# A new step order for a linear-attention and MLP kernel, from a plan in which engines take turns on a PSUM bank

## The chip, the core and the metric

The kernel runs on one core of a Trainium2 chip. The core has five engines that run their own instruction streams in order: TensorE (PE in the profile; its weight loads are shown as PEld), VectorE (DVE), ScalarE (ACT), GpSimd (POOL) and SyncE (SP, which here only issues DMAs). Matrix products land in PSUM, eight banks of 512 fp32 columns for each of 128 partitions; DVE and ACT carry results from there to SBUF. The metric is the device time of one execution in microseconds (us).

## The reference

A recurrent attention in the manner of RWKV-6 over 4 batches, 8 heads, 768 steps and heads of 48, followed by a token-mixing MLP:

```python
for t in range(S):                       # state: (B, H, 48, 48)
    cur = einsum('bhd,bhe->bhde', u[None] * kt, vt)
    y[:, :, t] = einsum('bhd,bhde->bhe', rt, state + cur)
    state = wt[:, :, :, None] * state + einsum('bhd,bhe->bhde', kt, vt)
x = y.transpose(0, 2, 1, 3).reshape(B, S, 384)
W_tok = 1/sqrt(64) * einsum('bsd,btd->bst', x @ w_q, x @ w_k)
out = relu(einsum('bst,btd->bsd', W_tok, x)) @ w_out
```

Inputs and output are fp32. All inputs together are 19.7 MB, and the output is 4.7 MB.

## The kernel before

The sequence is cut into units of 256 steps, three for each batch, so n runs from 0 to 11. A unit has two chunks of 128 steps. For each unit the function `unit` writes down some sixty steps. These are the ones that the rest speaks of, with their keys in the plan:

- **Loads** wg, kg, rg, vg (384 KB each, four buffers each, SP). For the last batch (units 9 to 11) v is loaded at once, as vw, in two steps of two DMAs.
- **ln** (ACT): log of the decay. **cw** (PE): running sums of it by a triangular matrix. **ep, en** (ACT): exp of plus and minus that sum, read from PSUM.
- **k16, r16, v16**: casts to bf16 (mostly POOL; k16 and r16 can also go to ACT).
- **kT, rT** (PE): transposes of k and r. Both land in one pair of PSUM banks, `kr`. For units 0 and 1 (`FULL`, line 245) k fills one bank and r the other; for all others each chunk has a bank that holds both.
- **ks** (ACT or DVE): copy of transposed k to SBUF. **qT** = r times ks, **RT** = r times ep (DVE, both read the `kr` banks), **KT** = ks times en (POOL or DVE; for units 0 and 11, `DIRECT`, DVE from the `kr` banks).
- **dps, dd, Vd**: the diagonal term, by PE, a copy of 16 columns, and a product on POOL. **vp, VB**: v in the order of steps, by PE and a copy; in the last batch VB is a POOL cast from vw.
- **A** (PE): scores of a chunk; **AM** (DVE): scores times the mask, 128x1024. **kb, kd**: KT turned back, by PE, and copied with a factor. **sn, SB**: the state, by PE and DVE. **yi, ya** (PE): output from the state and from the chunk. **X** (DVE): y scaled, plus Vd.
- **xt, XT**: X transposed and copied; **qk, QK**: the two projections and their copy.

At the end of a batch the MLP follows: **T** = k^T x by PE and **TS**, its copy; then for each unit **mx** (PE), **rl** (relu, to SBUF), **fp** (PE, with w_out), **os** (copy to SBUF) and **st** (store). In unit 11 (`end`) and the MLP of the last batch several steps are done in halves, one for each chunk.

The order is not that of the program text. `Plan` (lines 34 to 166) holds the steps with, for each engine that could do one, a time in ns. `order()` walks through the plan in planned time: each engine takes its steps by `RANK` (line 171, one number for each step); `ALT` (line 207) names, step by step, the engine for those that have a choice. A step may start when its engine is free, its inputs have ended, and a PSUM bank or ring buffer is free. `order()` also picks the banks (line 126). The steps are then issued in that sequence, so the plan fixes each engine's order and the banks; waits between engines come from the accesses. Thirty more steps, **z** (line 949), are fillers: a 128x512 product of zeros on PE, or nothing where `ALT` says `e`. Nine such products also stand in `setup`.

`begun` (line 415) gives the planned time at which each engine is through with the set-up. Clearing of buffers (`pads`, `kdz`) and `us`, `idu`, `gk` are DVE steps of the plan's start; `ub` copies the transposed u.

Of the kernel before, what the change touches and what calls it, by code (L numbers as in the profile page):

```python
# [33 lines left out]
class Plan:  # L34
# [4 lines left out]
    LAND = 1950  # L39

# [6 lines left out]
    def add(self, key, engs, fn, after=(), buf=None, reads=(), lag=None, mode=0, behind=None):  # L47
        opts = {}
        for e, x in engs.items():
            x = x if isinstance(x, tuple) else (x, mode, None)  # L50
            own = (260 if e in "Ee" else 80) if lag is None else lag
            opts[e] = (e.upper(), x[0], own, x[1], x[2])
        e = next(iter(opts)) if len(opts) == 1 else next(self.alt, "")
        e = e if e in opts else next(iter(opts))
        eng, dur, own, mode, kind = opts[e]
        if kind is not None:
            buf.kind = kind
        s = dict(key=key, opts=opts, way=e, eng=eng, dur=dur, fn=fn, lag=own, mode=mode, rank=0,
                 behind=behind, after=list(after), buf=buf, reads=list(reads), i=len(self.steps))
        if buf is not None:  # L60
            if buf.filler is None:
                buf.filler = s
                s["fill"] = buf.kind
                if behind is None:
                    s["behind"] = self.last.get(buf.kind)
                if buf.kind in self.rings:
                    self.last[buf.kind] = s
            else:
                s["fill"] = None
                if behind is None:  # L70
                    s["behind"] = buf.filler
        else:
            s["fill"] = None
        for b in reads:
            b.readers.append(s)
        self.steps.append(s)
        return s
# [8 lines left out]
    def order(self):  # L86
# [12 lines left out]
        owners, moved, done, mode = [None] * 8, [], [], 0  # L99

# [5 lines left out]
        def start(s):  # L106
# [9 lines left out]
            if s["fill"] in ("w", "s"):  # L116
                two = s["fill"] == "w"
                at = [clear(x) for x in owners]
                end = 7 if two else 8
                t = max(t, min(max(at[x:x + 1 + two]) for x in range(end)))  # L120
                if t >= never:
                    return never, None

                def beside(x):
                    return (x > 0 and at[x - 1] <= t) + (x < end - 1 and at[x + 1 + two] <= t)
                x = min((x for x in range(end) if max(at[x:x + 1 + two]) <= t),
                        key=lambda x: (beside(x), x if two else -x))
                return t, (x, 1 + two)
            if s["fill"] is not None:
                ring, size = rings[s["fill"]], self.rings[s["fill"]]  # L130
                if len(ring) >= size:
                    t = max(t, clear(ring[-size]))
            return t, None

        def run(s, t, took):
            s["start"], s["end"] = t, t + took + s["lag"]
            free[s["eng"]] = t + took
            done.append(s)

        while True:  # L140
# [16 lines left out]
            run(s, t, s["dur"] + self.SWITCH * change)  # L157
# [14 lines left out]
    0, 0, 0, 0, 2, 6, 4, 8, 5, 1, 17, 0, 0, 21, 2, 1, 5, 11, 0, 0, 0, 1, 0, 0, 2, 0, 0, 3, 0, 0,  # L172
    1, 3, 3, 4, 3, 4, 2, 5, 3, 4, 12, 6, 14, 10, 7, 12, 9, 5, 19, 9, 23, 12, 9, 10, 21, 16, 20,
    15, 13, 7, 15, 13, 27, 18, 37, 23, 29, 30, 31, 33, 22, 51, 22, 84, 35, 5, 0, 0, 4, 0, 0, 6,
    0, 0, 7, 0, 0, 8, 6, 7, 22, 10, 11, 24, 26, 17, 20, 21, 19, 8, 28, 14, 34, 16, 13, 38, 24,
    48, 28, 32, 15, 40, 26, 52, 29, 50, 53, 57, 61, 33, 76, 31, 92, 38, 8, 0, 0, 9, 0, 0, 10, 0,
    0, 11, 0, 0, 13, 11, 12, 35, 18, 17, 39, 42, 19, 27, 25, 15, 14, 49, 21, 58, 24, 18, 56, 31,
    63, 34, 55, 30, 60, 32, 67, 72, 68, 74, 37, 83, 42, 93, 39, 97, 41, 101, 44, 106, 47, 48, 0,
    0, 103, 45, 121, 54, 49, 0, 0, 126, 56, 138, 64, 52, 0, 0, 12, 0, 0, 13, 0, 0, 14, 0, 0, 15,
    0, 0, 20, 16, 17, 54, 23, 25, 64, 65, 26, 35, 36, 20, 19, 71, 28, 75, 32, 22, 78, 39, 82,  # L180
    41, 77, 38, 80, 40, 85, 43, 88, 90, 89, 91, 46, 105, 54, 111, 50, 16, 0, 0, 19, 0, 0, 20, 0,
    0, 21, 0, 0, 27, 34, 23, 73, 30, 29, 87, 94, 44, 48, 47, 45, 24, 95, 40, 100, 43, 29, 107,
    55, 99, 50, 96, 49, 104, 52, 110, 56, 115, 119, 117, 116, 60, 133, 59, 153, 69, 18, 0, 0,
    22, 0, 0, 23, 0, 0, 24, 0, 0, 33, 25, 26, 86, 37, 36, 98, 102, 42, 51, 53, 28, 27, 108, 49,
    109, 48, 30, 120, 61, 113, 58, 112, 57, 118, 59, 124, 129, 128, 127, 65, 134, 60, 155, 70,
    172, 77, 176, 79, 190, 86, 53, 0, 0, 178, 81, 205, 94, 51, 0, 0, 187, 84, 212, 97, 50, 0, 0,
    25, 0, 0, 28, 0, 0, 26, 0, 0, 29, 0, 0, 46, 31, 32, 114, 52, 53, 123, 125, 62, 64, 63, 36,
    33, 130, 58, 139, 63, 41, 141, 72, 136, 70, 135, 69, 140, 71, 143, 73, 147, 151, 152, 149,
    78, 163, 78, 177, 80, 27, 0, 0, 30, 0, 0, 31, 0, 0, 32, 0, 0, 51, 34, 35, 122, 55, 57, 131,
    132, 66, 68, 67, 39, 37, 137, 61, 148, 76, 45, 154, 80, 158, 82, 144, 74, 150, 77, 159, 81,  # L190
    169, 171, 173, 175, 91, 188, 85, 194, 88, 34, 0, 0, 33, 0, 0, 35, 0, 0, 36, 0, 0, 62, 38,
    40, 145, 67, 66, 142, 146, 65, 75, 79, 43, 42, 157, 72, 160, 83, 49, 174, 90, 165, 85, 164,
    84, 167, 86, 181, 184, 182, 183, 93, 189, 96, 206, 96, 215, 99, 229, 104, 238, 110, 54, 0,
    0, 234, 106, 246, 113, 55, 0, 0, 235, 120, 249, 115, 56, 0, 0, 37, 0, 0, 38, 0, 0, 40, 0, 0,
    42, 0, 0, 44, 0, 0, 68, 44, 46, 161, 74, 73, 168, 170, 87, 89, 88, 48, 51, 193, 99, 53, 192,
    98, 179, 92, 180, 82, 191, 97, 195, 101, 200, 203, 201, 202, 103, 213, 98, 222, 102, 39, 0,
    0, 41, 0, 0, 43, 0, 0, 71, 47, 50, 166, 76, 75, 185, 186, 83, 95, 94, 52, 54, 196, 100, 57,
    198, 102, 204, 104, 197, 89, 207, 105, 211, 108, 216, 218, 219, 220, 113, 226, 103, 232,
    105, 45, 0, 0, 47, 0, 0, 46, 0, 0, 87, 55, 56, 199, 92, 90, 93, 91, 208, 209, 95, 110, 107,
    106, 111, 109, 58, 221, 101, 59, 60, 214, 112, 225, 115, 217, 100, 223, 114, 224, 227, 228,  # L200
    230, 231, 233, 116, 236, 107, 239, 241, 108, 119, 117, 237, 118, 240, 245, 109, 111, 242,
    243, 244, 112, 121, 247, 122, 124, 250, 252, 125, 127, 57, 0, 0, 58, 0, 0, 248, 123, 114,
    253, 254, 128, 117, 59, 0, 0, 60, 0, 0, 251, 126, 116, 255, 256, 118, 129, 119, 130, 120,
    61, 0, 0, 43, 11, 44, 47, 6, 9, 45, 69, 62, 156, 25, 66, 18, 14, 10, 16, 59, 79, 36, 70, 41,
    2, 7, 210, 162, 81, 1, 8, 46, 17,
]
ALT = ("DPAEAAADEAAPPDDEAAEAEAAPPAPEAADEDAAAAAAAAPPAPEAAEDEDAAPDDeAAEDEAAPPAPEAADEAAAAAAAAAPPDPE"
       "AAEDEAAPPDPeADEDEAAPPAPEADDEDAAAAAADAPPDPDeAEAAPPAPDeAeAAPPAAAEAADEDAAADDDDDDADADAADADEE"
       "EEEEEEEEEEEEEEEEEEEEEeEEEEEE")
# [5 lines left out]
def kernel(  # L215
# [238 lines left out]
    def unit(n, batch):  # L454
# [71 lines left out]
        for cs in fine:  # L526
# [11 lines left out]
            x = add(("ep", n, cs[0]), {"A": 190 + int(w_ * 0.837)}, f_ep, [cws], ep, [cw])  # L538
            y = add(("en", n, cs[0]), {"A": 172 + int(w_ * 0.835)}, f_en, [cws], en, [cw])
# [8 lines left out]
        def transposed(name, src, step, place):  # L548
            def f(e):
                o = at(kr, BF16)  # L550
                for hp in range(NP):
                    for j in range(2):
# [10 lines left out]
                       mode=0 if full else 1)  # L563

        def turned(place, c0=0, nc_=2):
# [6 lines left out]
            e, view(ks.tile, 0, [[512, 2], [1, 512]]), turned(0)), [kTs], ks, [kr])  # L572
# [5 lines left out]
                  [rTs, kss], qT, [kr, ks])  # L578
# [3 lines left out]
        for cs in fine:  # L582
# [9 lines left out]
            def f_KT(e, cs=cs):  # L592
# [5 lines left out]
                else:  # L598
# [3 lines left out]
                    [rTs] + [eps[c] for c in cs], RT, [kr, ep])  # L602
            if n in DIRECT:
                y = add(("KT", n, cs[0]), {"D": 150 + int(n4 * C * 0.524)}, f_KT,
                        [kTs] + [ens[c] for c in cs], KT, [kr, en])
# [179 lines left out]
        for c in range(2):  # L785
# [6 lines left out]
            yas[c] = add(("ya", n, c), {"E": 205}, f_ya, [AMs[c], VBs], ys[c], [AM[c], VB])  # L792
# [96 lines left out]
        pieces = 2 if end else 1  # L889
# [4 lines left out]
        for ii in range(NU):  # L894
# [3 lines left out]
            def f_mx(e, ii=ii, mx=mx):  # L898
                for dt in range(NK):
                    mm(at(mx)[:, ds(dt * U, U)], TS.tile[:, ds(dt * 128, 128)],  # L900
                       view(QK.tile, ii * QS, [[64, 2], [C, 2], [1, 64]]),
                       start=(dt != 1))
# [5 lines left out]
            for cs in halves:  # L908
# [4 lines left out]
                    view(at(mx), cs[0] * C, [[U, NK], [1, w_]])), [mxs], MX, [mx])  # L913
            for cs in halves:
                def f_fp(e, cs=cs, fp=fp, MX=MX):
                    for c in cs:
                        for kt in range(NK):
# [4 lines left out]
                              fp, [MX])  # L922
            parts = 2 if end and ii == NU - 1 else 1
            for cs in halves:
# [5 lines left out]
                    [fps[cs]], o, [fp]) for x in range(parts)]  # L930
# [61 lines left out]
```

## Time and profile before

| | us |
|---|---|
| median of 3 runs | 106.54 (104.78 to 107.14) |
| profiled execution | 106.06 |
| its span, first to last instruction | 104.4 |

| group of the profile | count | busy us | mean ns |
|---|---|---|---|
| AM (DVE, 128x1024) | 24 | 29.1 | 1215 |
| KT (POOL, 128x1024) | 8 | 17.1 | 2132 |
| fillers Z (PE, 128x512) | 38 | 13.2 | 453 |
| fp (PE, 128x384) | 72 | 13.4 | 326 |
| ks on ACT / on DVE | 7 / 5 | 7.1 / 3.4 | 1018 / 686 |
| k casts on POOL / on ACT | 10 / 1 | 8.7 / 0.9 | 867 / 855 |
| os on ACT, 128x768 | 9 | 7.3 | 807 |

All DMA queues moved 24.66 MB; the queue of the loads and stores took 85.4% of the 16 DMA engines' time. The granted TensorE clock was 0.991 over the span.

How to read it: times are from one execution. A busy share says how much of a stretch an engine had an instruction running; a wait is idle time of an engine just before an instruction, put down to whatever ended last of the things it needed. A PE row ends when its pipeline has drained, so rows overlap, and the distance between starts is the better price of a step in a full stretch. On DVE and ACT too the next row starts up to about 0.1 us before the last one ends.

### The profile page before, as it was taken

How to read it: one execution, taken by the hardware profiler on the slowest of the kernel's cores; microseconds unless marked ns; L12 is line 12 of the kernel's file. 1: busy time of each engine (PE TensorE's matmuls, PEld its weight loads, DVE VectorE, ACT ScalarE, POOL GpSimd, SP SyncE). 2: the span in 40 equal slices, each digit the busy share in tenths (PEclk: the TensorE clock that was granted, in tenths of full speed). 3: DMA queues.
4: the chain of work that ended last, by engine and by line, in shares of the span. 5: the costliest groups of instructions: out<-in, count | busy, mean ns of one | idle time of the engine just before them, and what ended most of it. 6: DMA issues, size and time to landing. Idle time of an engine off the chain costs nothing.

```text
span 104.4 us, 4424 instructions
## 1 busy us (share of the span) xinstructions
PE 92.8 (89%) x1876; PEld 66.0 (63%) x1876; DVE 83.1 (80%) x145; ACT 80.4 (77%) x122; POOL 69.2 (66%) x80
## 2 busy tenths in 40 slices
PE   6999899979999998997998997999999879999920
PEld 2355568558577866675767865768686548766600
DVE  6256899598989999898998798899888497747820
ACT  6338896969799889996899759988989585765630
POOL 6486459896899859797979997396699705000000
PEclk9999999999999999999999999999999999999996
DMA  1999999999979999999979999999990039204693
GB/s 37 316 323 325 325 321 279 238 318 270 327 187 263 297 300 262 260 251 235 305 196 272 240 257 257 192 197 208 275 375 20 6 139 392 78 0 154 257 366 131
DMA packets 56403, 24.66 MB, mean 236 GB/s; under 512 B 54080, under 2 KB 55232, under 8 KB 56384
## 3 DMA queue, kind: packets, MB, share of 16 engines
q1 hardware_dynamic: 56224, 24.19, 85.4%
q8 instruction: 14, 0.23, 0.9%
q10 hardware_dynamic: 160, 0.20, 0.5%
q14 instruction: 5, 0.04, 0.1%
HBM read 19.66 MB, written 4.72 MB: 234 GB/s over the span
## 4 chain that ended last, share of the span: by engine, by line
PE 54%; POOL 11%; DVE 9%; ACT 8%; DMA 7%; issue 5%; SPq 2%; POOLq 0%; DVEq 0%; ACTq 0%
PE PS L254 54%; DMA vw<-in_v_dram 7%; POOL KT L600 5%; ACT ks L399 3%; DVE AM L687 2%; POOL Vd L667 2%; POOL r L490 2%; ACT kd L401 1%; DVE KT L600 1%; DVE ks L405 1%; SPq L307 1%; DVE X L804 1%; ACT en L535 1%; ACT ep L530 1%; SPq L314 1%
## 5 line engine op out<-in xcount | busy, mean ns | idle before, releaser
L687 DVE TENSOR_TENSOR AM<-PS,US 128x1024 bf16<-128x1024 f32 x24 | 29.1, 1215 | 0.8 <-PE PS L254 0.6
L667 POOL TENSOR_TENSOR Vd<-VB,dd 128x768 bf16<-128x768 bf16 (+1 forms) x14 | 18.5, 1325 | 7.0 <-issue 4.3
L600 POOL TENSOR_TENSOR KT<-ks,en 128x1024 bf16<-128x1024 bf16 x8 | 17.1, 2132 | 2.2 <-DVE ks L405 1.6
L535 ACT ACTIVATE en<-PS 128x1024 bf16<-128x1024 f32 (+1 forms) x14 | 12.4, 902 | 3.0 <-PE PS L254 2.6
L804 DVE SCALAR_TENSOR_TENSOR X<-PS,gx,Vd 128x768 bf16<-128x768 f32 (+1 forms) x13 | 12.4, 952 | 2.3 <-PE PS L254 2.1
L254 PE MATMUL PS<-Z 128*128 128x512 bf16 x38 | 13.2, 453 | 1.0 <-DVE Z L321 1.0
L254 PE MATMUL PS<-wo,MX 128*128 128x384 bf16 x72 | 13.4, 326 | 0.0
L530 ACT ACTIVATE ep<-PS 128x1024 bf16<-128x1024 f32 (+1 forms) x14 | 12.7, 924 | 0.5 <-PE PS L254 0.5
L254 PEld LDWEIGHTS <-KT 48*128 48x128 bf16 (+1 forms) x312 | 9.5, 94 | 4.8 <-issue 2.9
L479 ACT ACTIVATE lw<-wg 128x768 bf16<-128x768 f32 x12 | 10.2, 851 | 2.8 <-DMA wg<-in_w_dram 2.8
L590 DVE TENSOR_TENSOR RT<-PS,ep 128x1024 bf16<-128x1024 bf16 (+1 forms) x14 | 8.5, 606 | 4.0 <-ACT ks L399 2.6
L490 POOL CAST r<-rg 128x768 bf16<-128x768 f32 x12 | 9.9, 827 | 2.1 <-DMA rg<-in_r_dram 1.9
L490 POOL CAST k<-kg 128x768 bf16<-128x768 f32 x10 | 8.7, 867 | 1.9 <-DMA kg<-in_k_dram 1.0
L411 ACT ACTIVATE MX<-PS 128x768 bf16<-128x768 f32 (+1 forms) x10 | 7.5, 749 | 2.7 <-DVE MX L413 1.3
L399 ACT COPY os<-PS 128x768 f32<-128x768 f32 (+2 forms) x12 | 8.4, 698 | 1.5 <-PE PS L254 1.2
L254 PE MATMUL PS<-RT,KT 48*128 48x128 bf16 x192 | 9.4, 217 | 0.1
L254 PEld LDWEIGHTS <-MX 128*128 128x128 bf16 x72 | 6.5, 98 | 3.8 <-issue 0.2
L399 ACT COPY ks<-PS 128x1024 bf16<-128x1024 bf16 x7 | 7.1, 1018 | 2.4 <-DVE KT L597 1.2
L621 POOL CAST v<-vg 128x768 bf16<-128x768 f32 x9 | 7.5, 829 | 2.2 <-PE PS L254 1.1
L254 PE MATMUL PS<-CM,lw 64*128 64x128 bf16 x192 | 8.0, 224 | 0.4 <-DVE kd L407 0.4
L575 DVE TENSOR_TENSOR qT<-PS,ks 128x1024 bf16<-128x1024 bf16 x12 | 8.2, 681 | 0.3 <-PE PS L254 0.2
L254 PE MATMUL PS<-SB,RT 48*128 48x48 bf16 x160 | 7.0, 182 | 1.5
(89 smaller groups left out, 195.5 us busy)
## 6 DMA issues: line engine op xcount, KB each, us to landing
wg<-in_w_dram SPq DMA_DIRECT2D x12, 384.0 KB, 5.9
kg<-in_k_dram SPq DMA_DIRECT2D x12, 384.0 KB, 5.6
rg<-in_r_dram SPq DMA_DIRECT2D x12, 384.0 KB, 5.7
vg<-in_v_dram SPq DMA_DIRECT2D x9, 384.0 KB, 5.5
out_dram<-os SPq DMA_DIRECT2D x9, 384.0 KB, 3.2
vw<-in_v_dram SPq DMA_DIRECT2D x4, 288.0 KB, 6.0
out_dram<-os SPq DMA_DIRECT2D x5, 192.0 KB, 2.5
wof<-in_moe_w_out_dram SPq DMA_DIRECT2D x1, 576.0 KB, 6.2
```

Of the source, the lines that this page charges most:

```text
L254: return nc.tensor.matmul(o, l, rr, start=start, stop=stop, skip_group_check=True, is_transpose=trans)
L399: nc.scalar.copy(o, i)
L479: nc.scalar.activation(view(lw.tile, 0, [[64, H], [512, 2], [1, D]]), view(g["wg"].tile, 0, [[D2, H], [D, 2], [1, D]]), ACT.Ln, bias=0.0, ...
L490: op(view(o.tile, 0, [[64, H], [512, 2], [1, D]]), view(g[src].tile, 0, [[D2, H], [D, 2], [1, D]]))
L530: nc.scalar.activation(view(ep.tile, cs[0] * NP * EW + 66, [[EW, NP * len(cs)], [-65, 2], [1, 64]]), at(cw)[:, ds(cs[0] * 512, w_)], ACT.E ...
L535: nc.scalar.activation(en.tile[:, ds(cs[0] * 512, w_)], at(cw)[:, ds(cs[0] * 512, w_)], ACT.Exp, bias=0.0, scale=-1.0)
L575: lambda e: nc.vector.tensor_tensor(view(qT.tile, 0, [[512, 2], [1, 512]]), turned(second), view(ks.tile, 0, [[512, 2], [1, 512]]), ALU.mult),
L590: nc.vector.tensor_tensor(o, x, y, ALU.mult)
L600: x.tensor_tensor(o, view(ks.tile, cs[0] * 512, dims), y, ALU.mult)
L667: nc.gpsimd.tensor_tensor(Vd.tile[:, cols], VB.tile[:, cols], view(dd.tile, cs[0] * H, [[1, len(cs) * H], [0, D]]), ALU.mult)
L687: AMs[c] = add(("AM", n, c), {"D": 1221}, lambda e, c=c, A=A: nc.vector.tensor_tensor(view(AM[c].tile, 0, [[C, 8], [1, C]]), view(at(A), 0 ...
L804: nc.vector.scalar_tensor_tensor(view(X.tile, (2 * i + c0) * DM, [[DM, nc_], [1, DM]]), view(at(y), 0, [[512, nc_], [1, DM]]), gx, view(Vd ...
```

## The change

`Plan` is changed in five ways, and the step order and choice of engines were searched anew with it:

- A step that reads or writes a PSUM bank may, in the plan, only start when the other engines' last steps on that bank have ended (`used`, `banks`). `part` says which of a pair of banks a step touches, if only one.
- `OVER`: on ACT, DVE and POOL 100, 80 and 42 ns of a step's time are counted as overlapping the next step; its result comes as late as before, plus `AFTER`.
- `AFTER`: the time from a step's end to its users, by engine, in place of 260 for PE and 80 for all others.
- `COLD`: PE steps that start before 6,500 ns take twice as long in the plan.
- `RANK` and `ALT` have new values throughout.

Two edits change the instructions themselves. The copies that the last batch made in two pieces on two engines, TS and os of the last unit, are one piece again (os is still one for each chunk). And mx of the last batch writes its two chunks to two banks, as 18 matmuls of 128 columns in place of 9 of 256, where both chunks were spread over both banks before; relu reads accordingly.

```diff
+    COLD = 6500
+    OVER = dict(A=100, D=80, P=42)
+    AFTER = dict(E=200, A=80, D=62, P=65, S=80)
...
-            own = (260 if e in "Ee" else 80) if lag is None else lag
-            opts[e] = (e.upper(), x[0], own, x[1], x[2])
+            own = self.AFTER[e.upper()] if lag is None else lag
+            over = self.OVER.get(e, 0) if fn is not None else 0
+            opts[e] = (e.upper(), x[0] - over, own + over, x[1], x[2])
...
+        used = [{} for _ in range(8)]
+
+        def banks(s):
+            b = s["banked"]
+            if b is None or b.kind == "s" or s["part"] is None:
+                return [] if b is None else range(b.bank, b.bank + 1 + (b.kind == "w"))
+            return [b.bank + s["part"]]
...
+                t = max([t] + [y for x in banks(s) for e, y in used[x].items() if e != s["eng"]])
...
-            run(s, t, s["dur"] + self.SWITCH * change)
+            took = s["dur"] + self.SWITCH * change
+            run(s, t, took * (2 if e == "E" and s["fn"] and t < self.COLD else 1))
...
-        pieces = 2 if end else 1
+        pieces = 1
...
+                    x = TS.tile[:, ds(dt * 128, 128)]
+                    if end:
+                        for j in range(2):
+                            mm(at(mx)[:, ds(j * 512 + dt * C, C)], x,
+                               view(QK.tile, ii * QS + 64 * j, [[C, 2], [1, 64]]),
+                               start=(dt == 0))
+                        continue
...
-            parts = 2 if end and ii == NU - 1 else 1
+            parts = 1
```

What the new lists do, counted in the two built programs:

| step | before | after |
|---|---|---|
| ks on ACT / DVE | 7 / 5 | 2 / 10 |
| k16 on POOL (a half of unit 0 on DVE in both) / ACT | 11 / 1 | 7 / 5 |
| r16 on POOL / ACT | 12 / 0 | 11 / 1 |
| QK on ACT / DVE | 11 / 0 | 8 / 3 |
| XT on ACT / DVE | 9 / 4 | 11 / 2 |
| kd on ACT / DVE | 5 / 8 | 7 / 6 |
| rl on ACT / DVE | 10 / 5 | 8 / 7 |
| os on ACT / DVE | 12 / 5 | 14 / 1 |
| fillers z on PE / left out | 29 / 1 | 27 / 3 |

Among the orders that move: on DVE the k cast of unit 0 now stands ahead of `us`, `pads` and one `kdz`, and ks of unit 0 ahead of its KT. On PE one filler stands between kT and rT of unit 0, where six stood; the last filler is before rT of unit 3, where the last two stood among the steps of units 8 and 9. On POOL, KT of unit 10 comes before VB of unit 9, not after it. On SP, wg is loaded earlier against the other inputs, and the store of unit 3 comes before those of units 0 to 2.

## The prediction

> **What bounds the kernel now.** I read the busy shares first, then the stretches of the run, the waits of VectorE (DVE) between 7.5 and 75 us, the chain of waits, and the timeline of DVE at the start.
>
> The page's busy times (us, share of the span, instructions):
>
> ```profile
> PE 92.8 (89%) x1876; PEld 66.0 (63%) x1876; DVE 83.1 (80%) x145; ACT 80.4 (77%) x122; POOL 69.2 (66%) x80
> ```
>
> No engine is full over the span. By stretches (busy us of each engine, clock, DMA share, GB/s):
>
> ```profile
> 10.00:40.00 30.00, 28.27 (x641) 20.41 (x637) 27.39 (x40) 26.06 (x38) 24.08 (x24) 1.00 1.06 285
> 40.00:75.00 35.00, 32.29 (x775) 24.54 (x767) 31.55 (x47) 30.63 (x43) 28.99 (x25) 1.00 1.02 241
> 75.00:100.00 25.00, 23.27 (x416) 16.78 (x412) 18.57 (x34) 18.10 (x34) 9.44 (x9) 1.00 0.46 169
> 90.00:100.00 10.00, 9.88 (x87) 6.30 (x84) 6.67 (x14) 6.54 (x16) 0.00 (x0) 1.00 0.36 138
> ```
>
> Until 75 us TensorE (PE), DVE and ScalarE (ACT) are each some 90% busy: four in-order engines hand work to each other, and the stretch is as long as its fullest engine plus that engine's waits. PE's share there is flattered: 17 fillers (matmuls of zeros) stand after the first real A, about 0.22 us apart, and hide PE's waits. DVE, with no filler, has the least slack: 2.61 + 3.45 = 6.06 us. From 90 us on PE is full, and nothing but PE matters until its last matmul.
>
> What DVE waited for between 7.5 and 75 us (total us, times, longest):
>
> ```profile
> DVE RT L590 <- ACT ks L399: 1.5, 2, 1.1
> DVE RT L590 <- PE PS L254: 1.3, 2, 0.8
> DVE kd L407 <- PE PS L254: 0.9, 2, 0.5
> DVE X L804 <- PE PS L254: 0.8, 2, 0.4
> DVE kd L407 <- ACT kd L401: 0.5, 1, 0.5
> ```
>
> RT does not read ks. It reads the r half of the pair of banks whose k half ACT is copying into ks, so the first line is a wait for a turn on a bank. The end shows the same thing, beside the stretch that decides unit 9 (chain of waits; start us, us, what):
>
> ```profile
> 64.69 1.04 SPq L307
> ...
> 66.82 6.78 DMA vw<-in_v_dram
> ...
> 73.90 0.83 POOL VB L615
> 74.73 2.10 POOL KT L600
> ...
> 99.92 0.33 ACT os L399
> ...
> 100.27 0.36 DVE os L405
> ```
>
> The last two are the halves of one PSUM bank: DVE starts when ACT has ended. GpSimd (POOL) holds KT of unit 10 behind VB of unit 9, which waits for a load.
>
> The timeline of DVE at the start (start us, us; in brackets the idle time before it):
>
> ```profile
> 7.58 0.42 DVE L597 TENSOR_TENSOR KT<-PS,en 128x512 bf16<-128x512 bf16 x1 [0.95 <-ACT en L535]
> 9.53 0.42 DVE L590 TENSOR_TENSOR RT<-PS,ep 128x512 bf16<-128x512 bf16 x1 [0.83 <-PE PS L254]
> 10.81 0.42 DVE L407 TENSOR_SCALAR kd<-PS,gk 128x384 bf16<-128x384 bf16 x1 [0.45 <-ACT kd L401]
> 20.87 0.69 DVE L590 TENSOR_TENSOR RT<-PS,ep 128x1024 bf16<-128x1024 bf16 x1 [1.06 <-ACT ks L399]
> ```
>
> **The sum, on DVE.** The profiled execution took 106.06 us: a span of 104.4 and 1.66 around it, which I leave as it is. The median of the runs is 106.54, so the same change ends 0.5 us further from the median than from the profiled run. DVE's rows overlap, so I price a step by the distance of starts where DVE did not wait (AM 68.66 to 69.79: 1.13; ks 0.60; kd 0.54, its half 0.33; XT 0.47).
>
> *Waits that go.* (a) RT of unit 0 waited 0.83 for the r transposes, which stood behind six fillers (7.51 to 8.81 on PE); in the new order one filler stands between the k and the r transposes. (b) kd of unit 0: DVE takes the first half before ACT's, so the 0.45 falls on ACT. (c) ks of ten units is now on DVE, where it was on DVE in five; ACT keeps ks only for units 8 and 11. That removes RT's waits behind ks of unit 2 (1.06) and unit 10 (0.44). Together 2.78 us.
>
> *Waits that shrink.* The rest, 6.16 by the rows less 2.78, is 3.38 us, nearly all behind PE. PE in turn waited for DVE, ACT and POOL (SB 1.5, ks 0.5 and 0.3, kd 0.4, KT 0.3). POOL loses four k casts of 0.87 and one r cast of 0.83, 4.3 us of its 69.2, and does KT of unit 10 before VB of unit 9, so that the vw load no longer holds it. The bounds are 0 and 3.38; I take two thirds, 2.25, because POOL's lateness is what PE and the load slots hang on between 53 and 77 us.
>
> *Work that DVE gains*, units 0 to 10: four ks at 0.60 (2, 3, 5, 10; that of unit 0 is counted below); QK of unit 6, about 0.47 (an estimate by the XT copy of 0.47 and ACT's 0.48 for QK); relu of unit 2, 0.87 (row 0.95 less the overlap); two dd copies 0.16; kd of unit 9, 0.54. It loses three XT copies (1.41), three half kd (0.99), and pads and UB between KT and RT (0.46). Sum +1.58.
>
> *A wait that is added on DVE.* The k cast of unit 0 is now the first planned step and waits for its load (5.40 us as before). Behind it queue us, pads and one more clearing of kd, which lay in the idle time before 5.40. They are 0.25 + 0.42 + 0.68 = 1.35 us, so gk ends at 7.98 instead of 6.63; ks follows, and KT of unit 0 starts near 8.6 instead of 7.58: +1.0. A wait for ACT (0.95) gave most of the cover and is used up.
>
> *Casts on ACT.* ACT gains four k casts (0.86) and an r cast (0.84), two XT (0.80), two half kd, and loses five ks (1.02) and three QK (0.48): with os and relu about +0.1 of 80.4. Its sum costs nothing; the places might (second rival).
>
> *PE.* Two fillers fewer, 0.4 us, in idle time: nothing. The 256-wide matmuls of the last mx become 18 of 128 columns; equal columns, starts about 0.06 us apart as in the X transposes (six in 0.50) against 0.11: nothing. The ways of kb, vp and xt shift by a few matmuls: nothing.
>
> *The end.* os of the last chunk was 0.33, then 0.36, with a store behind both: 100.63 less 99.92 is 0.71. One ACT copy of 384 columns is 0.48: −0.22. ACT does all six last half copies; each PE group ahead takes 0.49, so it keeps up. TS in one piece instead of two turns saves as much, but lies behind fp of unit 7 (PE is full there): nothing. The stores' order changes, after all loads in both: nothing.
>
> Sum: −2.78 − 2.25 + 1.58 + 1.0 − 0.22 = −2.67, so 103.4 us.
>
> Which measure of PE is right bears on this. By the rows PE idles 11.6 us of the span and is full at the end. The Trainium skill (Perfetto Trace Analysis, "Identifying the Most-Contended Engine") calls matmul busy time a poor measure and takes that of weight loads: 63%, which would leave 38 us of slack and make a much larger gain possible. Between 90 and 100 us the trace disagrees: weight loads fill 6.30 us of 10, yet the matmuls stand back to back and carry the chain. I keep the rows.
>
> **Rivals.**
>
> *DVE becomes the bound (no change).* If PE-released waits merely return as other waits, only the named ones go: −2.78 + 1.58 + 1.0 − 0.22 = −0.4, 105.6. For it: DVE's 83.1 grows, and 40 to 75 us has only 3.45 idle. Against it: DVE is the chain for 9% only. It includes that the change does not do what it says: the build made the engines take turns already, and a re-ranked list that replaces each wait by an equal one gives 106.06.
>
> *Casts hold ACT (slower).* ACT is in order, and k of unit 2 now waits there for its load, with VB, ln, kd and en behind it, and through en and kd the whole unit. POOL's casts waited for loads up to 1.55 us (r), ACT's ln up to 1.8. At 1.1 us for each of five casts it is +5.5; against −2.67 that is +2.8: 108.9. It ends slower than before from 0.53 us a cast. Against it: from unit 3 on loads landed well before use, and wg now comes earlier in the queue.
>
> *All waits go.* Every DVE wait (−6.16), +2.58, −0.22, and PE's wait of 1.04 at 83 us behind SB: −4.8, 101.2.
>
> *The clock falls.* The last filler now stands before r of unit 3; before, two stood at 61 and 63 us. At the start eleven fillers take 4.87 us, 0.44 apart, twice the 0.22 of later ones: a PE that has not run is half as fast. If a wait sent it back for as long, 4.9 us would do the work of 2.4: +2.4, 105.8. From 35 to 100 us the longest wait of PE was 1.04 us and no row shows that pace again, with two fillers, so it hardly decides. The Trainium skill (TensorE: Matmul & The Clock Gate, "What's actually happening") names about 3.4 us of idleness for the fall; no run here shows one.
>
> **Chances.** Forecast 0.52, centre 103.4; DVE bound or nothing done 0.25; ACT held 0.10; all waits go 0.10; clock 0.03. About 2% (2.1 us; 104.4 and 108.7) is what can be told from no change here. The forecast's own range is 102.3 (all 3.38 go) to 104.9 (a quarter goes); about a sixth of its chance lies above 104.4. Faster: 0.43 + 0.10 = 0.53. Same: 0.09 + 0.25 + 0.03 (clock) = 0.37. Slower: 0.10. The range is 101.2 (all waits go) to 107.0 (the casts hold ACT by 0.72 us each, +3.6 − 2.67); it leaves out the held ACT at its full price and what lies below 101.2.
>
> **What would show it.** Right: no RT behind ks before unit 8; AM of unit 0 near 11.0 instead of 11.74 although KT starts later; DVE idle under 3 us between 10 and 75; KT of unit 10 well before 74.7; one os copy at the end. Wrong: DVE idle unchanged with other names, or ACT idle before k casts, released by DMA. What would overturn it: PE less busy than 9.5 of 10 us in the last stretch.

## The result and the profile after

| | before | after |
|---|---|---|
| median of 20 runs each, us | 105.34 (104.41 to 107.14) | 104.03 (103.26 to 105.5) |
| ratio after to before | | 0.9887, 95% interval 0.9851 to 0.9922 |
| profiled execution, us | 106.06 | 103.3 |
| its span, us | 104.4 | 101.6 |

The change makes the kernel 1.1% faster, within the 2% that count as no change. Ratios here and below leave out executions more than 1.5% above the fastest of the same kernel, the profiled one of before among them, while medians and ranges hold all. The two profiled executions are 2.76 us apart because that of before lies above its median and that of after below; typical executions are 1.2 to 1.3 us apart. A difference read between the two profiles must therefore be checked against other executions of the same order.

The page's busy times after (us, share of the span, instructions):

```profile
PE 90.9 (90%) x1881; PEld 65.5 (64%) x1881; DVE 84.2 (83%) x146; ACT 80.6 (79%) x123; POOL 64.9 (64%) x75
```

POOL has lost 4.3 us and five instructions, DVE has gained 1.1. By stretches of after (busy us of PE, weight loads, DVE, ACT, POOL; then clock, DMA share, GB/s):

```profile
10.00:40.00 30.00, 27.79 (x615) 19.71 (x614) 27.37 (x41) 24.78 (x35) 21.70 (x21) 1.00 1.07 290
40.00:75.00 35.00, 33.57 (x837) 26.05 (x830) 33.42 (x51) 33.64 (x48) 31.07 (x26) 1.00 1.05 252
75.00:100.00 25.00, 21.84 (x381) 16.25 (x379) 17.62 (x30) 16.94 (x33) 6.23 (x7) 1.00 0.49 186
```

From 10 to 40 us DVE is idle for 2.63 us, as before (2.61). From 40 to 75 us it is idle for 1.58 instead of 3.45. What DVE waited for between 7.5 and 75 us in after (total us, times, longest):

```profile
DVE ks L426 <- PE PS L275: 1.1, 3, 0.6
DVE SB L772 <- PE PS L275: 0.9, 2, 0.5
DVE AM L713 <- PE PS L275: 0.8, 2, 0.5
DVE qT L599 <- PE PS L275: 0.4, 2, 0.2
DVE RT L614 <- PE PS L275: 0.3, 1, 0.3
```

No line names ACT any more; all waits are now for PE. The start of the run in after, by the timeline of DVE:

```profile
8.04 0.68 DVE L426 COPY ks<-PS 128x1024 bf16<-128x1024 bf16 x1
8.64 0.41 DVE L621 TENSOR_TENSOR KT<-PS,en 128x512 bf16<-128x512 bf16 x1
8.97 0.41 DVE L614 TENSOR_TENSOR RT<-PS,ep 128x512 bf16<-128x512 bf16 x1
10.56 0.40 DVE L428 TENSOR_SCALAR kd<-PS,gk 128x384 bf16<-128x384 bf16 x1
10.95 1.22 DVE L713 TENSOR_TENSOR AM<-PS,US 128x1024 bf16<-128x1024 f32 x1
```

KT starts 1.06 later than before, and AM 0.79 earlier, with nothing idle between. And the chain of waits of after (start us, us, what):

```profile
10.15 6.02 DMA wg<-in_w_dram
...
16.25 0.85 ACT lw L500
...
25.61 0.09 DVE dd L426
...
25.84 1.47 POOL Vd L693
27.31 0.77 POOL v L647
28.08 1.26 POOL r L511
...
29.38 4.58 PE PS L275 x98
...
85.73 11.53 PE PS L275 x131
...
97.28 0.48 ACT os L420
```

The chain now runs from a load of unit 2 over POOL's Vd of unit 2, which waits for dd, to the cast of r of unit 3 queued behind it. The load vw and POOL's VB, on the chain of before from 65.7 to 74.7 us, are off it.

**Where the time went.** I cut the traces at three products AM, which every kernel has: the first in time of unit 5, the first of unit 10 and the last of unit 11. The table also holds the traces of the experiments below; "old" and "new" is the order of the steps, and in the last two rows steps of the new order are put back.

| trace | order | start to unit 5 | unit 5 to 10 | unit 10 to 11 | rest of span |
|---|---|---|---|---|---|
| before | old | 44.56 | 32.96 | 10.67 | 16.2 |
| b_again | old | 44.44 | 31.63 | 10.68 | 16.2 |
| b_half_v | old | 44.53 | 31.65 | 10.67 | 16.2 |
| b_pieces | old | 44.43 | 32.41 | 10.68 | 16.2 |
| b_ks_dve | old, ks moved | 44.26 | 32.22 | 10.17 | 16.2 |
| b_ks_dve_2 | old, ks moved | 44.22 | 33.10 | 10.18 | 16.2 |
| b_ks_pieces | old, ks moved | 44.87 | 32.13 | 10.17 | 16.0 |
| after | new | 44.77 | 31.12 | 9.63 | 16.1 |
| a_half_v | new | 44.96 | 31.67 | 9.63 | 16.1 |
| a_start | new | 44.94 | 31.91 | 9.63 | 16.1 |
| a_wg2 | new | 44.65 | 31.53 | 9.63 | 16.1 |
| a_wg2_r3 | new | 44.36 | 32.55 | 9.64 | 16.7 |
| a_ks_act | new, ks back | 49.75 | 31.52 | 9.66 | 16.6 |
| a_pool_casts | new, casts back | 51.15 | 32.12 | 10.82 | 15.9 |

Three things stand in it. Up to unit 5 the change gains nothing. From unit 5 to 10 the time varies by 1.4 to 1.5 us in either order, so the 1.84 us between the two profiles there cannot be told from two different executions. From unit 10 to 11 each order repeats to 0.01 us, and the new one is 1.04 shorter; of the last two rows one repeats the new order to 0.03, and the other, a_pool_casts, has lost the gain (see there). PE has about as much to do there: the profiles have 229 matmul records in that stretch in both, though not all of the same steps (before still holds the transposes of unit 11's k, after the sums cw of unit 11), and PE is busy for 9.41 us before and 9.31 after, so its idle time fell from 1.26 to 0.32. (Less fillers, the first stretch has some 19 records fewer in the new order and the second 11 more, so these two are compared to within a us.) With the last stretch (16.2 to 16.1) that makes 1.1 to 1.2 us, the difference of typical executions.

What happens between unit 10 and unit 11 is seen on DVE. Before (timeline of DVE; in brackets the idle time ahead and what ended it):

```profile
81.73 0.42 DVE L597 TENSOR_TENSOR KT<-PS,en 128x512 bf16<-128x512 bf16 x1 [0.28 <-PE PS L254]
83.29 0.42 DVE L590 TENSOR_TENSOR RT<-PS,ep 128x512 bf16<-128x512 bf16 x1 [1.14 <-ACT ks L399]
83.63 0.35 DVE L746 TENSOR_TENSOR SB<-PS,ep 128x192 bf16<-128x192 f32 x1
```

and of ACT and PE in the same execution:

```profile
82.25 1.01 ACT L399 COPY ks<-PS 128x1024 bf16<-128x1024 bf16 x1 [1.20 <-DVE KT L597]
...
84.03 0.49 PE L254 MATMUL PS<-ID,X 128*128 128x128 bf16 x6 [1.04 <-DVE SB L746]
```

DVE, ACT and DVE take turns on the banks of unit 11's k and r: ks waits for KT, RT waits for ks, SB stands behind RT, and PE has nothing to do for 1.04 us. After, ACT's copy, still on ACT, is ahead of en and long done (ACT, then DVE):

```profile
76.83 1.02 ACT L420 COPY ks<-PS 128x1024 bf16<-128x1024 bf16 x1
```

```profile
79.25 0.68 DVE L599 TENSOR_TENSOR qT<-PS,ks 128x1024 bf16<-128x1024 bf16 x1
79.85 0.42 DVE L621 TENSOR_TENSOR KT<-PS,en 128x512 bf16<-128x512 bf16 x1
80.18 0.79 DVE L614 TENSOR_TENSOR RT<-PS,ep 128x512 bf16<-128x512 bf16 x2
```

Nothing waits, and PE is busy for 11.71 of the 12 us from 78 to 90, where it was 10.52. Before first, then after:

```profile
78.00:90.00 12.00, 10.52 (x241) 7.91 (x241) 9.21 (x15) 9.06 (x16) 6.58 (x8) 1.00 0.38 145
```

```profile
78.00:90.00 12.00, 11.71 (x238) 9.10 (x231) 11.23 (x19) 7.93 (x14) 3.23 (x4) 1.00 0.24 90
```

### The profile page after: what moved, and what is told of

Same layout as the page of the kernel before. It is cut to its first block, busy times and chain, and to the rows that moved or that the text cites. A ratio compares the mean times of both kernels' runs of the same rounds, so it can differ in the third digit from the quotient of the medians.

```text
span 101.6 us, 4422 instructions
## 1 busy us (share of the span) xinstructions
PE 90.9 (90%) x1881; PEld 65.5 (64%) x1881; DVE 84.2 (83%) x146; ACT 80.6 (79%) x123; POOL 64.9 (64%) x75
## 4 chain that ended last, share of the span: by engine, by line
PE 57%; DVE 10%; SPq 9%; ACT 7%; DMA 6%; POOL 3%; issue 3%; DVEq 0%; ACTq 0%; POOLq 0%
PE PS L275 57%; SPq L328 9%; DMA wg<-in_w_dram 6%; DVE AM L713 5%; ACT lw L500 2%; POOL Vd L693 1%; DVE ks L426 1%; DVE qT L599 1%; ACT os L420 1%; POOL r L511 1%; ACT QK L420 1%; ACT ep L551 1%; DVE X L831 1%; DVE SB L772 1%; ACT XT L420 1%
## 5 line engine op out<-in xcount | busy, mean ns | idle before, releaser
L275 PEld LDWEIGHTS <-KT 48*128 48x128 bf16 (+1 forms) x304 | 10.0, 94 | 4.7 <-issue 2.7
L275 PE MATMUL PS<-Z 128*128 128x512 bf16 x36 | 11.9, 435 | 1.0 <-DVE Z L342 1.0
L420 ACT COPY os<-PS 128x768 f32<-128x768 f32 (+1 forms) x14 | 9.3, 663 | 2.7 <-PE PS L275 2.6
L420 ACT COPY XT<-PS 128x768 bf16<-128x768 bf16 (+1 forms) x11 | 8.5, 771 | 0.5 <-ACT en L556 0.2
L772 DVE TENSOR_TENSOR SB<-PS,ep 128x192 bf16<-128x192 f32 x20 | 7.0, 351 | 1.4 <-PE PS L275 1.4
L275 PE MATMUL PS<-CM,lw 64*128 64x128 bf16 x192 | 7.5, 217 | 0.8 <-ACT lw L500 0.8
L275 PE MATMUL PS<-VB,AM 128*128 128x48 bf16 x192 | 8.2, 184 | 0.0
```

The costliest lines, as they stand in the source:

```text
L275: return nc.tensor.matmul(o, l, rr, start=start, stop=stop, skip_group_check=True, is_transpose=trans)
L420: nc.scalar.copy(o, i)
```

## The experiments

Three theories stood against each other in turn. "Turns": the gain is that four copies ks, and with them DVE's turns behind ACT, leave ACT. "POOL relief" or "loads": it is that POOL's casts and the loads behind them leave the chain. "Search": it is the new order as a whole, and no part of it alone. All runs below are compared with the kernel before on the same chip.

Steps were moved by two lines in the plan, with a table of engines and ranks for the steps named:

```diff
-        e = e if e in opts else next(iter(opts))
+        e = WAY.get(key, e) if e in opts else next(iter(opts))
...
-            s_["rank"] = x
+            s_["rank"] = AT.get(s_["key"], x)
```

**b_again**, the kernel before unchanged, for a second trace.

> The kernel before, unchanged, profiled a second time. The first profile had a span of 104.4 us in a run of 106.06, while the median is now 105.34; there the eleven fillers at the start took 4.87 us and the first cw began at 5.84, in the profile of the changed kernel they took 4.18 and cw began at 5.14, though neither order nor number of these matmuls changed. Theory 'phase': the start differs from run to run; a second profile can show cw at 5.1 to 5.9 and the span follows by less than that, 103 to 104.5. Rival 'order': cw of unit 0 is late in the kernel before for a reason of its order, and starts at 5.84 again.

It took 104.78 us. At the start the same eleven fillers and the sums cw behind them ran faster (cw at 5.29 instead of 5.84 us), and AM of unit 0 came only 0.11 earlier for it: of the faster start little is left there. What differs most is POOL from 47 to 56 us. Before (POOL's timeline):

```profile
49.34 0.83 POOL L490 CAST r<-rg 128x768 bf16<-128x768 f32 x1 [0.36 <-DMA rg<-in_r_dram]
...
53.73 0.83 POOL L490 CAST k<-kg 128x768 bf16<-128x768 f32 x1 [0.70 <-PE PS L254]
54.52 2.14 POOL L600 TENSOR_TENSOR KT<-ks,en 128x1024 bf16<-128x1024 bf16 x1
```

and b_again, the same casts:

```profile
48.59 0.83 POOL L490 CAST r<-rg 128x768 bf16<-128x768 f32 x1
...
52.23 0.83 POOL L490 CAST k<-kg 128x768 bf16<-128x768 f32 x1
53.02 2.13 POOL L600 TENSOR_TENSOR KT<-ks,en 128x1024 bf16<-128x1024 bf16 x1
```

A load of r came late in one execution and not in the other, a cast behind it then waited for PE too, and KT is 1.50 us apart. (In that line the wait is put down to what came last.)

**b_pieces**: the kernel before in its old order, but TS and os copied whole, and the last mx in two banks.

```diff
-        Ts = [add(("TS", n, x), ..., lambda e, x=ds(x * w_, w_): copy(e, TS.tile[:, x], at(T)[:, x]), ...)
+        Ts = [add(("TS", n, x), ..., lambda e, x=x: x == 0 and copy(e, TS.tile[:, ds(0, DM)], ...), ...)
```

> The kernel before with the edits of instructions alone: TS and os of the last unit in one piece, mx of the last batch with a bank for each chunk, the old order. Theory (forecast): only the end of the last os matters, 0.71 us becomes 0.48, so -0.2 us of 105.3: ratio 0.998, and PE as full as before from 90 us on. Rival: the pieces and the mixed banks held PE up in the tail, and a good part of the 1.1% is here: ratio 0.992 or less.

0.9934 (0.9885 to 0.9982), between the two expectations. Its trace has the old 10.68 us from unit 10 to 11. From the last AM to the end of the last copy it has 12.10 us, where before has 12.44 and after 12.24, so the pieces are worth 0.2 to 0.3 us up to there. Little of this reaches the end: the rest of the span is 16.2 us as before. And the medians, 106.0 and 106.06, show no gain, so the 0.7% is not shown to be one.

**b_ks_dve** and its repetition **b_ks_dve_2**: the kernel before, old order, with four ks on DVE.

```diff
+WAY = {('ks', 2): 'D', ('ks', 3): 'D', ('ks', 5): 'D', ('ks', 10): 'D'}
+AT = {('ks', 2): 24.5, ('ks', 3): 33.5, ('ks', 5): 50.5, ('ks', 10): 93.5}
```

> The kernel before with ks of units 2, 3, 5 and 10 moved from ACT to DVE and nothing else. Theory 'turns': RT's waits for ACT's ks of units 2 and 10 (1.06 and 0.44 us) go, ACT loses 4 x 0.93 us, DVE gains 4 x 0.60; DVE loses 1.5 us of waits and gains 2.4 of work, ACT gets room: between -1.0 and +0.9 us, 0.3 faster if I must say one: ratio 0.997. Rival 'search': moving single steps without re-ranking the rest only shifts waits; DVE is the fullest engine, so +1 to +2.4 us: ratio 1.01 to 1.02.

> b_ks_dve once more (the kernel before with ks of units 2, 3, 5 and 10 on DVE, old order), since b_ks_pieces, which has it and more, measured 0.999 on another chip. If four ks on DVE are worth 1.1% by themselves: 0.985 to 0.993 again. If the 0.9893 was owed to a chip on which the kernel before is slow (its median there was 106.06, in the other comparisons 105.3 and 105.7), and the gain of the kernel after needs the new order: 0.995 to 1.002, about 105.0 us on any chip.

0.9893 (0.9838 to 0.9947) on one chip and 0.9991 (0.9916 to 1.0066) on another. The wait of RT behind ks of unit 2 is gone in both, and the first AM of unit 2 comes 0.67 and 0.70 us earlier than before; by unit 5, 0.30 and 0.34 are left, and by unit 10 the two are 1.04 and 0.20 ahead of the profile of before and both behind b_again. Why the first ratio is the lower one is not shown. Of the 17 executions of the kernel before that it is taken against none was under 105.43 us, though b_again took 104.78 on the same chip; on the other chip the fastest was 104.61. In unit 11, not edited, the turn fell otherwise: ACT copied ks ahead of KT. DVE's timeline of b_ks_dve_2:

```profile
82.49 0.42 DVE L601 TENSOR_TENSOR KT<-PS,en 128x512 bf16<-128x512 bf16 x1 [1.26 <-ACT ks L403]
82.84 0.41 DVE L594 TENSOR_TENSOR RT<-PS,ep 128x512 bf16<-128x512 bf16 x1
```

One wait in place of two, and the stretch from unit 10 to 11 is 10.18: half of the gain there without any new order. From the last AM to the end of the last copy both then take 12.68 us for the 12.44 of before, so half of that half is lost again. Alone, the four ks are worth little that can be told.

**b_ks_pieces**: both of these edits together.

> The kernel before in its old order and with its old engines, but for the two parts that measured best alone: ks of units 2, 3, 5 and 10 on DVE, and TS and os copied whole with two banks for the last unit's mx. If the two gains are separate, 0.9893 x 0.9934 = 0.983, below the kernel after (0.9887), and nothing of the gain is owed to the new order. If they are the same slack counted twice, 0.989. Rival 'search' (part of the gain is owed to the new order): 0.990 or more. The last copy out should take 0.48 us as in the kernel after, not 0.71.

0.999 (0.9912 to 1.0069). Not the sum of the two gains and not the gain of one; it goes with the second run of b_ks_dve. "Search" was nearest. The last copies out are as expected: three of them stand back to back in 1.41 us.

**a_ks_act**: the kernel after with the same four ks back on ACT.

```diff
+WAY = {('ks', 2): 'A', ('ks', 3): 'A', ('ks', 5): 'A', ('ks', 10): 'A'}
+AT = {('ks', 2): 18.5, ('ks', 3): 24.5, ('ks', 5): 40.5, ('ks', 10): 81.5}
```

> The changed kernel with ks of units 2, 3, 5 and 10 put back on ACT, nothing else moved. Theory 'turns': RT and qT wait again for a turn on the bank pair behind ACT's 0.9 to 1.0 us, and ACT, 33.64 us busy of 35 between 40 and 75 us, has no room: +1.0 to +2.5 us, ratio to before 0.998 to 1.01 (the changed kernel: 0.989). Rival 'ks is indifferent': DVE is relieved by 2.4 us and that pays for the turns: 0.985 to 0.993.

1.026 (1.0181 to 1.0339), slower than any theory had it. ACT is in order, and here ks of unit 5 (42.27 us, 1.01) went ahead of TS, for which PE waited. PE's timeline of a_ks_act:

```profile
43.72 0.50 PE L279 MATMUL PS<-QK,TS 128*128 128x256 bf16 x3 [1.49 <-ACT TS L424]
```

Then the clock fell (see the end). What an undone part costs is thus the price of a step out of place in an order made without it, not the worth of the part.

**a_pool_casts**: the kernel after with five casts back on POOL.

```diff
+WAY = {('k16', 2): 'P', ('k16', 3): 'P', ('k16', 7): 'P', ('k16', 11): 'P', ('r16', 4): 'P'}
+AT = {('k16', 2): 11.5, ('k16', 3): 13.5, ('r16', 4): 19.5, ('k16', 7): 29.5, ('k16', 11): 50.5}
```

> The kernel after, with five casts given back to POOL: k16 of units 2, 3, 7 and 11 (ACT and DVE have them in the kernel after) and r16 of unit 4, at the places of the old order. All else stays. POOL gets 5 x 0.83 = 4.15 us back, 64.9 to about 69 us. Theory 'turns' (the gain is that four ks left ACT's queue; b_ks_dve, which does that alone in the old order, measured 0.9893): POOL has slack, the ratio to the kernel before stays at 0.985 to 0.992, the place of the kernel after. Rival 'POOL relief' (the gain of the kernel after is that POOL is no longer on the chain with its casts, loads and KT from 53 to 77 us): back to 0.996 to 1.004. Rival 'fit' (a searched order and its engines belong together, so that one part undone costs whatever it is, as in a_ks_act with 1.026): over 1.005, with a wait in front of PE that neither kernel has.

1.0664 (1.0575 to 1.0753), with two new waits in front of PE ("fit"). Waits of PE in a_pool_casts:

```profile
PE PS L279 <- POOL r L515: 3.7, 2, 2.8
PE PS L279 <- POOL k L515: 2.1, 1, 2.1
```

On POOL the cast of k of unit 2 stands behind a cast of v that waited 1.68 us for its load, and that of r of unit 4 behind KT, which waited 2.32 us for DVE. The run says that the new order needs these casts off POOL, and nothing on whether the old one did.

The stretch from unit 10 to 11 is 10.82 us here, and its reason is a third wait. ACT still copies ks of unit 11 ahead of en, and DVE waits for no turn, but the cast of its k is late (POOL, then PE's weight loads):

```profile
83.46 0.83 POOL L515 CAST k<-kg 128x768 bf16<-128x768 f32 x1
```

```profile
84.34 0.29 PEld L279 LDWEIGHTS <-k 64*128 64x128 bf16 x16 [1.29 <-POOL k L515]
```

PE transposes k as soon as POOL has cast it, and had been idle for 1.12 us. In after ACT casts this k at 70.59. So in the new order the gain there also needs this cast early; b_ks_dve, with the cast on POOL, has half of it.

**a_start**: us, kdz and pads of DVE's start put back ahead of the first k cast.

```diff
+AT = {('us',): 0.4, ('kdz', 1): 0.5, ('pads',): 0.6}
```

> The kernel after, with us, kdz and pads of the start put ahead of DVE's k cast of unit 0, where the kernel before has them. My forecast charged their new place with 1.0 us. By it KT of unit 0 comes from 8.64 us to about 7.9, the first AM from 10.95 to about 10.3, and if that carries to the end the ratio is 0.981 to 0.984. Rival 'the start is bound by loads' (the chain of the kernel after runs from the tenth load, wg of unit 2, landed at 16.25 us): AM moves, the end doesn't, 0.985 to 0.992.

0.9891 (0.9823 to 0.9958), the place of the kernel after. KT came to 8.10, but RT then waited for en, and AM started where it had. In this execution PE's sums cw and with them the first en came 1.03 us later than in the profile of after (7.00 for 5.97), so the rows do not price the move; that nothing is gained at the end rests on the ratio. The timeline of DVE in a_start:

```profile
8.69 0.42 DVE L616 TENSOR_TENSOR RT<-PS,ep 128x512 bf16<-128x512 bf16 x1 [0.18 <-ACT en L558]
...
10.99 1.23 DVE L715 TENSOR_TENSOR AM<-PS,US 128x1024 bf16<-128x1024 f32 x1
```

**a_wg2** and **a_wg2_r3**: the kernel after with the load of wg of unit 2 one place earlier (and the k cast of unit 2 later on ACT), and the same with POOL's r cast of unit 3 ahead of Vd of unit 2.

```diff
+AT = {('wg', 2): 7.5, ('k16', 2): 14.5}                      # a_wg2
+AT = {('wg', 2): 7.5, ('k16', 2): 14.5, ('r16', 3): 14.5}    # a_wg2_r3
```

> The kernel after, with the load of wg of unit 2 issued one place earlier on SP, ahead of kg of unit 2, and that unit's k cast after its ln on ACT. If the load of wg sets the chain at the start, ln of unit 2 begins some 1.1 us before 16.25 (one issue on SP is 1.15 us), POOL's Vd of unit 2 and with it r16 of unit 3 and PE's wait for it at 29.4 us come forward, and if that carries to the end the ratio is 0.977 to 0.983. Rival 'the start is slack' (the times of AM show nothing gained or lost before 45 us, and before and after differ only between 45 and 85 us): 0.985 to 0.992.

> a_wg2 (the load of wg of unit 2 one place earlier, 0.983), and POOL's r16 of unit 3 ahead of its Vd of unit 2, which in a_wg2 still waits 2.2 us for a load of v queued ahead of it. If the start carries to the end, PE's wait for r of unit 3 near 29.3 us goes, 1 to 2 us more come off, 0.965 to 0.975. If what is gained at the start is taken back by 72 us by the rate of the loads: 0.980 to 0.988, like a_wg2.

0.983 (0.9769 to 0.9892) and 0.9908 (0.9854 to 0.9962). In a_wg2 the chain moved to the load of kg of unit 2, landed at 16.27, and r of unit 3 was cast at 27.89 instead of 28.02. In a_wg2_r3 that cast came at 24.44, and AM of unit 5 0.41 earlier than in after. The profiled execution then took 32.55 us from unit 5 to 10 and kept nothing. Neither is shown to beat the kernel after.

**a_half_v** and **b_half_v**: both kernels with half of five loads of v left out.

```diff
-                                     lambda e, ap=ap, x=g[name].tile: load(b, i, x, ap),
+                                     lambda e, ap=ap, x=g[name].tile, h=H // 2 if name == "vg" and n > 3 else H:
+                                     load(b, i, x, ap, h),
```

> The kernel after, with half of v's heads left out of the loads of units 4 to 8 (the units from 4 on that load v by themselves): 5 x 192 KB, 0.98 MB less, and what those heads compute is of older data. Everything on the engines stays. In the traces the 16 DMA engines are busy at 1.0 and more from 10 to 70 us and move 285 to 299 GB/s at best, and 0.98 MB at 285 GB/s is 3.4 us. Theory 'loads' (to about 72 us the kernel goes at the rate of its loads, and what a good order gains is DMA time that isn't idle): 1.7 to 3.4 us off, 0.955 to 0.972 of the kernel before. Rival 'engines' (DVE and ACT, 95% busy from 40 to 75 us, and their waits set the pace, as my forecast had it): less than 0.8 us off, 0.981 to 0.990.

> The same for the kernel before: the same five loads halved, nothing else. The trace of before has 250 GB/s from 40 to 60 us, and POOL waits there for loads of r and k (0.36 and 0.59 us). Theory 'loads': 1.7 to 3.4 us off, 0.968 to 0.984. Rival 'engines': less than 0.8 us off, 0.992 to 1.0.

0.9829 (0.9753 to 0.9904) and 0.992 (0.9874 to 0.9965). Neither kernel goes at the rate of its loads: of 3.4 us of DMA time at most about a quarter came off. But for the kernel before, 0.8% came off, and nine of its ten runs lie between 104.66 and 105.54 (the tenth took 108.44), while the full kernel ran from 104.61 to 108.3 there. Its trace repeats b_again within 0.1 us in each stretch of the table. So late loads cost the old order about 0.8% (0.4 to 1.3 by the interval). For the kernel after the interval overlaps that of its own ratio, and whether it loses less to them is open. And b_half_v keeps the wait that I had priced highest. Of its waits of DVE, 7.5 to 75 us:

```profile
DVE RT L591 <- ACT ks L399: 1.5, 2, 1.1
```

## Why the prediction was right, and where it was not

The median of 104.03 lies in the range of 101.2 to 107.0, and the way is the one that was forecast. The class, within 2%, was given 0.37, and "faster" 0.53. The sum behind the time was right in sign and double in size: −2.67 against 1.2 to 1.3 us of typical executions. That the profiled execution of after took 103.3, next to the 103.4 forecast, is luck: it is set against a profile of before from one of its longer executions. And the total is closer than its terms, since two that came to nothing stand beside one that was left out. (By the sum's own terms "a quarter goes" gives 104.8 and not 104.9.) Its terms, in their order:

- **Waits that go, −2.78.** They went: no ACT in DVE's list, AM of unit 0 at 10.95 for the 11.0 promised. But they gave nothing to the end. Up to unit 5 the new order is 0.21 slower. b_ks_dve removes the waits of units 2 and 10 for 0.9991 and 0.9893, and b_half_v keeps them and is faster. The step that failed is "the stretch is as long as its fullest engine plus that engine's waits": I took DVE's waits for the path though DVE was on the chain for 9% only. In after, DVE waits for PE instead, and PE for r of unit 3 (0.38 us, with a filler ahead), behind a POOL step that waited 2.52 us for dd.
- **Waits that shrink, −2.25.** Not there by name: what DVE waits for PE between 7.5 and 75 us is 3.9 us, where the lines of before give 3.7. DVE idle from 10 to 75 us is 4.21, not under 3, and was 6.06.
- **Work that DVE gains, +1.58.** Up to the first AM of unit 10, DVE is busy for 67.28 us after and 66.15 before, +1.13; from 0 to 100 us it is +1.66. It holds a gain that I had not seen: KT on DVE took 0.68 twice instead of 1.12 and 1.16 (below).
- **The start, +1.0.** KT at 8.64 for the 8.6 worked out. a_start takes it back, and the ratio stays (0.9891 for 0.9887): it costs nothing that the runs show.
- **Casts on ACT.** Cost nothing, as said; no wait for a load of k or r is among ACT's longer waits in after. The rival of a held ACT fell. Moved back, the casts cost 6.6%, a matter of the order. What the sum had no term for is that one of them, k of unit 11, is what lets ks of unit 11 go early.
- **The end, −0.22.** The last copy took 0.48 for 0.71, and PE was full up to it. From the last AM to the end of that copy it is 12.24 for 12.44: the term was right for the copy, but the span from that AM on is only some 0.1 us shorter (16.1 for 16.2).
- **What I left out** is the term that carried: the turn on unit 11's banks. RT's third wait behind ks (1.14 at 83.29) and PE's wait of 1.04 behind it stood in the trace, and I had both in hand, but I closed my view of DVE at 75 us and wrote that ACT "keeps ks only for units 8 and 11" as if that left unit 11 as it was. The 1.04 stood only in the rival in which all waits go. It is the same mechanism that I named, turns on a bank, at the place where PE had nothing else to do. That this turn is worth about 1 us rests on the chain of before, which runs from KT over ks, RT and SB to PE (81.73 to 84.03 us), on the stretch that repeats to 0.03 us in each kind of row but the last, and on b_ks_dve, where the turn fell half right and half was gained there. It is not isolated: in after the k transposes of unit 11 come before the stretch too, and a_pool_casts shows that the new order loses the gain when they come late. Moving ks of unit 11 alone in the old order was not tried.
- **POOL.** That KT of unit 10 would leave the load vw came true (71.03 instead of 74.73 us), and 1.84 us lie between the two profiles from unit 5 to 10. b_again, with KT behind VB as before, has 1.33 of them too. So most of this is the profiled execution of before, with a load that came late in it, and only what after has over b_half_v's 31.65, about half a us, could belong to the change.

The first rival (only the named waits go, 105.6) was off as well: what went was a wait that was not among the named.

## What to carry to other kernels

Price a wait by what PE, or whichever engine is full to the end, lost to it; a long wait of another engine is worth nothing until that engine is shown to be on the path, and a short one late in the run may be worth all of itself. Take a second trace of the same kernel before subtracting two: here one stretch of one kernel varied by 1.33 us and another repeated to 0.01. And do not read the worth of a part from undoing it in a searched order, since 2.6% and 6.6% were lost by undoing parts of a change worth 1.1%.

## What the hardware showed unexpectedly

**DVE and POOL hold each other up, and the earlier one keeps its time.** The product KT from two SBUF tensors on DVE took 0.68 us or up to 1.16, by when POOL's cast beside it began. Before (DVE, then POOL):

```profile
35.27 1.16 DVE L600 TENSOR_TENSOR KT<-ks,en 128x1024 bf16<-128x1024 bf16 x1
```

```profile
35.06 0.83 POOL L621 CAST v<-vg 128x768 bf16<-128x768 f32 x1 [0.28 <-POOL r L490]
```

b_again, the same two instructions of the same kernel:

```profile
35.15 0.69 DVE L600 TENSOR_TENSOR KT<-ks,en 128x1024 bf16<-128x1024 bf16 x1
```

```profile
35.19 1.33 POOL L621 CAST v<-vg 128x768 bf16<-128x768 f32 x1 [0.53 <-DMA vg<-in_v_dram]
```

Where POOL began 0.21 us earlier, KT is 0.47 longer; where DVE began 0.04 us earlier, the cast is 0.50 longer. The Trainium skill (SBUF — State Buffer, "Who interferes with whom") says so: a DVE instruction with two SBUF inputs contends with a GpSimd instruction that reads SBUF. The trace agrees. It also says that the order of issue decides who blocks, which these rows bear out. They show less than a full block, though POOL's times in a profile are rough: in before the cast had 0.62 us left when KT began, and KT lost 0.47.

**The clock fell after a wait of 1.49 us, and not after one of 2.83.** In a_ks_act PE was idle from 42.23 to 43.72; the granted clock (third figure from the end) then stood at half. Stretches of 1 us:

```profile
43.00:44.00 1.00, 0.28 (x3) 0.21 (x3) 0.00 (x0) 1.00 (x3) 0.64 (x1) 1.00 1.05 293
...
45.00:46.00 1.00, 1.00 (x33) 0.90 (x28) 0.93 (x1) 0.28 (x2) 0.48 (x1) 0.50 0.99 274
46.00:47.00 1.00, 1.00 (x21) 0.66 (x19) 1.00 (x3) 1.00 (x2) 0.00 (x0) 0.50 1.09 290
...
48.00:49.00 1.00, 1.00 (x23) 0.76 (x21) 0.17 (x1) 0.45 (x2) 1.00 (x1) 1.00 1.09 273
```

It lasted from 44.5 to 48.0 us (from 44 to 45 us the mean is 0.77). In a_pool_casts a wait of 2.14 us (to 19.93) was followed by such a fall from 21.8 to 25.2, and one of 2.83 us (to 40.56) by none. So the length of a wait alone does not decide. The prediction's rival of a falling clock did not come in the kernel after, but its price, work at half speed, for 3.4 us each time, is what these two kernels paid. The Trainium skill (TensorE: Matmul & The Clock Gate, "What's actually happening") lets the clock fall after an idle window of about 3.4 us that runs freely, not started by the kernel. That the place of the wait counts agrees with these rows; that a whole window must be idle does not, since the clock fell after 1.49 us.
